# Sigmoid attention and a two-layer MLP: quarter matmuls gathered beside every second block, and PSUM banks shared between scores and sums

## The chip, the cores and the metric

The kernel runs on one core of a Trainium2 chip. The metric is the time of the program on the device in microseconds, the median of the runs shown. Engines: TensorE (PE; its weight loads are listed as PEld), VectorE (DVE), ScalarE (ACT), GpSimd (POOL), SyncE (SP), which issues the DMAs.

## The reference

Batch 8, 12 heads, sequence 448, head dimension 64; then an MLP of 768 x 2048 x 768 over the 3584 rows.

```python
scores = scale * np.matmul(q, k.transpose(0, 1, 3, 2)) - np.log(S)
attn = 1.0 / (1.0 + np.exp(-scores))
x = np.matmul(attn, v)                # heads joined: (3584, 768)
h = x @ w_in
r = np.maximum(h, 0.0)
out = (r * r) @ w_out
```

## The kernel before, in words

The kernel has two parts. The first, of about 252 us, is the attention, and beside it the conversion of the MLP's weights (they arrive as 64-bit words) into float32 blocks and the sums that the second part needs. The second part, the MLP, multiplies in a seven-product scheme; the change does not touch it.

The attention runs over 48 pairs of heads. A block `d` (0 to 23) treats the pairs `n = 2d` and `n + 1`. The order of the instructions on each engine is that of the program text, written out by hand; a tile waits for a free buffer of its kind, and each engine's queue is in order.

The 448 keys of a head are three tiles of 128 and a rest of 64. TensorE does four kinds of work in a block, in three forms:

- scores (`scores`, tile `sc`, L276): two heads side by side, each on 64 of the 128 rows ("64*128"). Six score tiles per block, three for each pair, of two PSUM banks each; three passes for each tile, `qh qh`, `qh ql`, `ql qh`: x is split into a high and a low part. A sigmoid on ScalarE (L259) reads each tile out into `at`.
- the scores of the rests (`scores_rest`, tile `sr`, L292): quarters, "64*64", for the two pairs of the *next* block, with a sigmoid of their own into `rest`.
- the rests' part of the sums (`attn_v_rest`, tile `pav`, L304): quarters, which open the sums of this block.
- the sums over the full key tiles (`attn_v`, tile `pav`, L313): halves, "128*64", 24 records a block.

PSUM has eight banks: three score tiles of two banks (tag `sc`) and one tile `duo` of two, which takes one score tile of each block (the fourth) and then the block's two sums. The next block begins with `put`: VectorE copies the two sums out (L322, `xo`).

VectorE does in each block, in this order: a step of the weight conversion (`weights_join`), the high part of one x (`high`, L489), the two copies (`put`), its low part (`low`, L493), at some blocks parts of the MLP's operands (`later`, `pieces`), a second high part, a second step of conversion, its low part. Steps of the conversion are numbered `k`; of three, two are conversions (`convert_join`, L152, L153, L156 on VectorE, then an add on GpSimd, L159), and one makes the four sums of a block of weights (`sums`, L168 to L171), which read what GpSimd added. ScalarE does the first half of a conversion (`convert_words`, L147, L148). `weights_of(piece, n)` runs the steps that fall on pair `n`: nearly always one.

SyncE's queue takes the loads of x (five to six pairs ahead), of v (one block ahead), of the weights, and the stores. x, v, `at`, `rest` and the high and low parts share 35 buffers (`op2`).

Before the loop, eight matmuls on zeros run while the first x is loaded (in two pieces).

Of the kernel before, what the change touches and what calls it, by code (L numbers as in the profile page):

```python
# [8 lines left out]
F32 = mybir.dt.float32  # L9
# [6 lines left out]
PSUM = bass.MemoryType.PSUM  # L16

B, H, S, D = 8, 12, 448, 64
DM, DFF = H * D, 2048
P = 128  # L20
# [42 lines left out]
DEFERRED = (5, 6, 7)  # L63


PIECES = {12: (1,), 14: (2,), 18: (3,), 21: (6,)}
T_PIECES = {17: ("t1",), 21: ("t2",), 23: ("t3",)}


# [1 line left out]
def sigmoid_attention_relu2_mlp(  # L71
# [171 lines left out]

    def load_pair(b, p):
        x = op2(f"x_{b}_{p}")
        to, src = (t.rearrange("p a s -> p (a s)") for t in (x, qk[b, p]))

        for at, end in ((0, S + P), (S + P, 2 * S)) if (b, p) == (0, 0) else ((0, 2 * S),):
            nc.sync.dma_start(out=to[:, at:end], in_=src[:, at:end])
        return x  # L250

    def load_v(b, d):
        vt = op2(f"v_{b}_{d}").rearrange("p a s -> p (a s)").rearrange("p (t d) -> p t d", d=P)
        nc.sync.dma_start(out=vt, in_=v[b, d])
        return vt

    def sigmoid(name, sc):
        at = op2(name)
        nc.scalar.activation(at, sc, AF.Sigmoid, bias=NEG_LOG_S, scale=SCALE)  # L259
        return at  # L260

    def score_tile(name):
        return ps.tile([P, 2, 512], F32, tag="sc", bufs=3, name=name)[:, :, :S]

    def scores(b, p, x, passes=((0, 0), (1, 0), (0, 1))):

        out = []

        other = (0, 2) if (b, p) >= (B - 1, NP - 2) else (1, 0)
        for t in range(NT):  # L270
            sc = (duo if (p % 2, t) == other else score_tile)(f"sc_{b}_{p}_{t}")
            ks = slice(t * P, (t + 1) * P)
            for n, (kp, qp) in enumerate(passes):
                for j in range(2):
                    rows = slice(j * D, (j + 1) * D)
                    nc.tensor.matmul(  # L276
                        sc[:, j],
                        x[kp][rows, 1, ks],
                        x[qp][rows, 0],
                        start=(n == 0),  # L280
                        stop=(n == len(passes) - 1),
                    )
            out.append(sigmoid(f"at_{b}_{p}_{t}", sc))
        return out

    def scores_rest(d, xs):

        sc = score_tile(f"sr_{d}")
        for r, x in enumerate(xs):
            for j in range(2):  # L290
                rows = slice(j * D, (j + 1) * D)
                nc.tensor.matmul(  # L292
                    sc[r * KR : (r + 1) * KR, j], x[rows, 1, NT * P :], x[rows, 0], start=True, stop=True
                )
        return sigmoid(f"rest_{d}", sc)

    def attn_v_rest(d, rest, vt):

        sums = duo(f"pav_{d}")
        pavs = [sums[:, r] for r in range(2)]  # L300
        for r in range(2):
            for j in range(2):
                rows, columns = slice(r * KR, (r + 1) * KR), slice(j * D, (j + 1) * D)
                nc.tensor.matmul(  # L304
                    pavs[r][columns], vt[rows, 2 * NT, columns], rest[rows, j], start=True, stop=False
                )
        return pavs

    def attn_v(n, pav, at, vt):
        for t in range(NT):  # L310
            for j in range(2):
                columns = slice(j * D, (j + 1) * D)
                nc.tensor.matmul(  # L313
                    pav[columns], vt[:, n % 2 * NT + t, columns], at[t][:, j], start=False, stop=(t == NT - 1)
                )

    def put_x(b, p, pav, scalar=False):
# [114 lines left out]
    def block(d):  # L432

        n = 2 * d
        more = n + 2 <= last
        for m in (n + 5, n + 6):
            load(m)
        if more:  # L440
            vt[d + 1] = load_v(*divmod(d + 1, NP // 2))
        for store in ready:
            store()
        ready.clear()
        if d == 0:
            for m in (1, 2, 3):
                high(m)
                low(m)
            score(0, (x[0],), ((0, 0),))
            rest[0] = scores_rest(0, (x[0], x[1]))  # L450
        else:
            weights_of(weights_join, n - 2)
            high(n + 3)
            put(n - 2)
            put(n - 1)
            low(n + 3)
            for piece in later:
                piece()
            later.clear()
            pieces_of(*T_PIECES.get(d, ()))  # L460
            score(n, xs[n])
        score(n + 1, xs[n + 1])
        if more:
            rest[d + 1] = scores_rest(d + 1, (x[n + 2], x[n + 3]))
        pav[n], pav[n + 1] = attn_v_rest(d, rest.pop(d), vt[d])
        for m in (n + 2, n + 3):
            weights_of(weights_load, m)
        high(n + 4)
        weights_of(weights_join, n - 1)
        low(n + 4)  # L470
        for m in (n, n + 1):
            weights_of(weights_words, m)
        if more:
            for store in stores:
                store()
            stores.clear()
        attn_v(n, pav[n], at[n], vt[d])
        attn_v(n + 1, pav[n + 1], at[n + 1], vt[d])
        for name in PIECES.get(d, ()):
            pieces[name](later)  # L480

    def load(n):
        if n <= last:
            x[n] = load_pair(*pairs[n])

    def high(n):
        if n <= last:
            xs[n] = op2(f"qh_{n}", F32R), op2(f"ql_{n}", F32R)
            nc.vector.tensor_copy(out=xs[n][0], in_=x[n])  # L489

    def low(n):
        if n <= last:
            nc.vector.tensor_sub(out=xs[n][1], in0=x[n], in1=xs[n][0].bitcast(F32))  # L493
# [7 lines left out]
    def weights_of(piece, n):  # L501
        for k in range(NK):
            if k * NWP // NK == n:
                piece(k)
# [19 lines left out]
    def duo(name):  # L524
        return ps1.tile([P, 2, 512], F32, tag="duo", bufs=1, name=name)[:, :, :S]
# [218 lines left out]
        return ahead  # L744

    with tc.manual_schedule():
        with tc.tile_pool(name="ps", bufs=3, space=PSUM) as ps:
            wp = ps.tile([P, 2, 512], F32, tag="sc", bufs=3, name="warm_ps")[:, :, :S]
            for i in range(8):
                nc.tensor.matmul(wp[:, 0], warm[:, :P], warm[:, :S], start=True, stop=True)  # L750
            load(0)
            load(1)
            vt[0] = load_v(0, 0)
            load(2)
            load(3)
            for k in range(2):
                weights_load(k)
            load(4)
            for d in range(len(pairs) // 2 - 2):
                block(d)  # L760
                if d == KEPT * NP // 2:
                    ops[0], made = x_operands(0)
                    pieces.update(made)
            load_first(0, False)
            block(len(pairs) // 2 - 2)
            load_first(0, True)
            for i in (1, 2):
                load_first(i, False)
            halve_weights(first[0, False])
            block(len(pairs) // 2 - 1)  # L770
            halve_weights(first[1, False])
            put(last - 1)
            put(last, True)
        ps2 = ctx.enter_context(tc.tile_pool(name="ps2", bufs=6, space=PSUM))
        work = [
            (0, lambda: pieces_of(7)),
            (1, lambda: halve_weights(first[0, True])),
            (2, lambda: pieces_of(5)),
            (4, lambda: halve_weights(first[2, False])),
            (5, lambda: pieces_of("t4")),  # L780
            (6, lambda: pieces_of(4)),
            (9, lambda: [store() for store in stores]),
        ]
        at_step = {s: n for n, s in enumerate(STEPS[0])}

        for (n, i), (j, late), wait in (
            [((7, 0), (1, True), 4), ((7, 1), (3, False), 4), ((4, 0), (2, True), 4)]
            + [((7, i), (i + 2, False), 4) for i in range(2, NI - 2)]
            + [((4, i), (i + 2, True), 4 if i < NI - 3 else 2) for i in range(1, NI - 2)]
        ):  # L790
            at_load = at_step[n, i]
            work.append((at_load, lambda j=j, late=late: load_first(j, late)))
            work.append((at_load + wait, lambda j=j, late=late: halve_weights(first[j, late])))
        for n, i in enumerate(DEFERRED):
            work += deferred(i, 10 + 12 * n)
        between = {}
        for n, piece in work:
            between.setdefault(n, []).append(piece)
        made = gemm1(0, ops[0], first, between)
# [40 lines left out]
```

## Time and profile before

| | |
|---|---|
| median of 3 runs | 1075.53 us (1075.03 to 1076.74) |
| the profiled execution | 1074.75 us, span 1072.9 us |
| TensorE busy | 1066.6 us, 99% |
| VectorE, ScalarE, GpSimd busy | 777.7, 608.8, 75.3 us |
| the attention, to the MLP's first matmul | 251.91 us |

Rows of a timeline give the start in us from the span's start, the duration from the first start to the last end of the merged instructions, engine, line, operation, tiles, shapes and count, and in brackets the idle time of the engine before it with what ended it. A matmul of these types is recorded more than once for each call in the code, and records overlap: the time that a step costs is the distance from start to start. "64*128" is the part of the array that a matmul uses, rows by columns.

### The profile page before, as it was taken

The numbers are of one execution on the slowest core, as the hardware profiler recorded it, in microseconds if no ns is written. First come the engines' busy times: TensorE is split into PE (matmuls) and PEld (weight loads), VectorE is DVE, ScalarE is ACT, GpSimd is POOL, SyncE is SP. The second block draws the span as 40 slices with busy tenths as digits, with TensorE's granted clock in tenths as the row PEclk, the third lists the DMA queues.
The fourth block names the chain that finished last, engine by engine and source line by source line (L and its number), as shares of the span: only waits on it lengthen the run. The fifth ranks groups of instructions, "written<-read, shape, count | busy, mean of one in ns | idle before, by whom it ended". The sixth has DMA issues, their size and how long they took to land.

```text
span 1072.9 us, 14947 instructions
## 1 busy us (share of the span) xinstructions
PE 1066.6 (99%) x5858; PEld 888.7 (83%) x5858; DVE 777.7 (72%) x888; ACT 608.8 (57%) x749; POOL 75.3 (7%) x42
## 2 busy tenths in 40 slices
PE   9999999999999999999999999999999999999998
PEld 4555555557999999999999999999999999999997
DVE  6888899876688898635579884456997925579941
ACT  6877778766766765433455654334565523455721
POOL 1322232210121000000000000000000000000000
PEclk9999999999999999999999999999999999999999
DMA  9989999791566445533342465333335633333441
GB/s 363 387 291 329 366 381 336 297 304 55 195 240 212 144 143 170 189 123 104 103 140 83 147 221 179 107 105 104 106 127 195 203 98 122 120 97 112 144 144 52
DMA packets 83446, 196.80 MB, mean 183 GB/s; under 512 B 6704, under 2 KB 57776, under 8 KB 83376
## 3 DMA queue, kind: packets, MB, share of 16 engines
q1 hardware_dynamic: 83376, 195.85, 52.9%
q8 instruction: 46, 0.75, 0.3%
q14 instruction: 24, 0.20, 0.1%
HBM read 154.53 MB, written 41.29 MB: 183 GB/s over the span
## 4 chain that ended last, share of the span: by engine, by line
PE 81%; DVE 2%; issue 0%; POOL 0%; ACT 0%; DVEq 0%; ACTq 0%
PE ha L534 22%; PE oa L534 22%; PE hb L534 11%; PE ob L534 11%; PE hc L534 5%; PE oc L534 5%; PE pav L313 2%; PE sc L276 2%; PE pav L304 0%; PE sr L292 0%; DVE a L152 0%; POOL a L159 0%; DVE qh L489 0%; DVE xo L322 0%; DVE ql L493 0%
## 5 line engine op out<-in xcount | busy, mean ns | idle before, releaser
L237 DVE TENSOR_TENSOR w_1l<-w_1l,w_1h 128x1536 fp32r<-128x1536 f32 x60 | 105.9, 1765 | 73.6 <-ACT w_1h L236 73.0
L259 ACT ACTIVATE at<-sc 128x896 f32<-128x896 f32 x144 | 119.6, 934 | 57.8 <-PE sc L276 57.8
L577 ACT COPY s<-ha 128x448 f32<-128x448 f32 x96 | 50.9, 531 | 132.2 <-PE ha L534 122.1
L313 PE MATMUL pav<-at,v 128*64 128x448 f32 x576 | 113.5, 543 | 0.0
L236 ACT CAST w_1h<-w_1l 128x1536 fp32r<-128x1536 f32 x60 | 88.8, 1481 | 19.2 <-DMA w_1l<-w 18.9
L313 PEld LDWEIGHTS pav<-at,v 128*64 128x64 f32 x576 | 39.2, 137 | 72.7 <-issue 71.0
L237 DVE TENSOR_TENSOR w_5l<-w_5l,w_5h 128x1152 fp32r<-128x1152 f32 x32 | 43.3, 1354 | 45.0 <-ACT w_5h L236 45.0
L159 POOL TENSOR_TENSOR a<-a,f 128x768 int32<-128x768 int32 x26 | 60.8, 2340 | 162.8 <-DVE a L156 52.5
L236 ACT CAST w_0h<-w_0l 128x1536 fp32r<-128x1536 f32 x28 | 41.5, 1481 | 50.6 <-DMA w_0l<-w 50.6
L237 DVE TENSOR_TENSOR w_0l<-w_0l,w_0h 128x1536 fp32r<-128x1536 f32 x28 | 49.1, 1755 | 19.4 <-ACT w_0h L236 19.3
L276 PE MATMUL sc<-qh 64*128 64x448 f32 x282 | 54.6, 383 | 1.6 <-DVE xo L322 1.6
L493 DVE TENSOR_TENSOR ql<-x,qh 128x896 fp32r<-128x896 f32 x47 | 54.8, 1166 | 0.1
L276 PE MATMUL sc<-qh,ql 64*128 64x448 f32 x282 | 51.8, 362 | 0.0
L276 PE MATMUL sc<-ql,qh 64*128 64x448 f32 x282 | 51.6, 361 | 0.0
L236 ACT CAST w_5h<-w_5l 128x1152 fp32r<-128x1152 f32 x32 | 37.1, 1159 | 25.2 <-DMA w_5l<-w 25.1
L614 DVE TENSOR_TENSOR g<-hb,s 128x448 f32<-128x448 f32 x32 | 19.9, 622 | 43.3 <-PE hb L534 43.3
L276 PEld LDWEIGHTS sc<-qh 64*128 64x128 f32 x282 | 26.7, 184 | 21.4 <-issue 14.7
L560 DVE SCALAR_TENSOR_TENSOR g<-g 128x896 f32<-128x896 f32 x40 | 43.6, 1090 | 1.1
L489 DVE CAST qh<-x 128x896 fp32r<-128x896 f32 x47 | 32.4, 690 | 8.5 <-DMA x<-qk 8.5
L702 ACT COPY t<-oa 128x448 f32<-128x448 f32 x36 | 19.1, 529 | 31.8 <-PE oa L534 31.5
L322 DVE COPY xo<-pav 128x448 f32<-128x448 f32 x47 | 27.2, 619 | 12.4 <-PE pav L313 12.2
L534 PE MATMUL oa<-o_0h,w_0h 128*128 128x448 f32 x96 | 35.1, 365 | 0.0
(522 smaller groups left out, 3062.0 us busy)
## 6 DMA issues: line engine op xcount, KB each, us to landing
w_1l<-w SPq DMA_DIRECT2D x60, 768.0 KB, 4.5
w_0l<-w SPq DMA_DIRECT2D x28, 768.0 KB, 4.5
x<-qk SPq DMA_DIRECT2D x47, 448.0 KB, 7.0
f<-w_in SPq DMA_DIRECT2D x16, 768.0 KB, 7.7
w_5l<-w SPq DMA_DIRECT2D x32, 384.0 KB, 3.9
v<-v SPq DMA_DIRECT2D x24, 448.0 KB, 7.4
outT<-o SPq DMA_DIRECT2D x47, 224.0 KB, 2.1
w<-s SPq DMA_DIRECT2D x13, 768.0 KB, 8.9
```

The source lines that it names most:

```text
L159: nc.gpsimd.tensor_tensor(out=wb, in0=wb, in1=t.bitcast(I32)[:, :, 0], op=ALU.add)
L236: nc.scalar.copy(out=hi, in_=raw)
L237: nc.vector.tensor_sub(out=lo, in0=raw, in1=hi.bitcast(F32))
L259: nc.scalar.activation(at, sc, AF.Sigmoid, bias=NEG_LOG_S, scale=SCALE)
L276: nc.tensor.matmul(sc[:, j], x[kp][rows, 1, ks], x[qp][rows, 0], start=(n == 0), stop=(n == len(passes) - 1),)
L313: nc.tensor.matmul(pav[columns], vt[:, n % 2 * NT + t, columns], at[t][:, j], start=False, stop=(t == NT - 1))
L322: nc.vector.tensor_copy(out=x, in_=pav)
L489: nc.vector.tensor_copy(out=xs[n][0], in_=x[n])
L493: nc.vector.tensor_sub(out=xs[n][1], in0=x[n], in1=xs[n][0].bitcast(F32))
L534: nc.tensor.matmul(out, a[:, c], b, start=first and n == 0, stop=last and n == 2, skip_group_check=True)
L560: nc.vector.scalar_tensor_tensor(out=t, in0=t, scalar=0.0, in1=t, op0=ALU.max, op1=ALU.mult)
L577: nc.scalar.copy(out=s, in_=banks["a", i])
```

## The change

- Quarters: those of four pairs run together, behind the halves of every even block: scores of the rests for blocks `d + 2` and `d + 3`, then the rests' part that closes the sums of block `d` and the part that opens those of `d + 1`. An odd block has no quarters. Blocks 0 and 1 begin this in a way of their own.
- Banks: two score tiles (`sc`) instead of three, and two tiles of sums: `even` and `odd` (the former `duo`), for the blocks of even and odd number. `LENT` says which of the six score tiles of a block (0 to 5) take one of them: in an even block the third takes `even` and the fourth `odd`; in an odd block, where `odd` holds opened sums, the third and the sixth take `even`.
- VectorE's order: the two copies come first in a block. The steps of the conversion move: three in an even block (one ahead of the first low part, two around the second high part), one in an odd one; on ScalarE one word step in an even block and three in an odd one. High and low parts are made one pair later, for the next block's pairs only.
- Loads: x is loaded eight and nine pairs ahead instead of five and six (blocks 0 and 1 load four each), v two blocks ahead instead of one. The first x comes in one piece, and there are nine matmuls on zeros.
- One piece of the MLP's operands moves from block 21 to 22.

```diff
-PIECES = {12: (1,), 14: (2,), 18: (3,), 21: (6,)}
+PIECES = {12: (1,), 14: (2,), 18: (3,), 22: (6,)}
...
     def score_tile(name):
-        return ps.tile([P, 2, 512], F32, tag="sc", bufs=3, name=name)[:, :, :S]
+        return ps.tile([P, 2, 512], F32, tag="sc", bufs=2, name=name)[:, :, :S]
+
+    def even(name):
+        return ps.tile([P, 2, 512], F32, tag="even", bufs=1, name=name)[:, :, :S]
+
+    def odd(name):
+        return duo(name)
+
+    LENT = {0: {2: even, 5: odd}, 1: {2: odd, 3: even}, 2: {2: even, 3: odd}, 3: {2: even, 5: even}}
...
-        other = (0, 2) if (b, p) >= (B - 1, NP - 2) else (1, 0)
+        d, at = divmod(b * NP + p, 2)
         for t in range(NT):
-            sc = (duo if (p % 2, t) == other else score_tile)(f"sc_{b}_{p}_{t}")
+            sc = LENT.get(min(d, 2 + d % 2), {}).get(at * NT + t, score_tile)(f"sc_{b}_{p}_{t}")
...
         n = 2 * d
-        more = n + 2 <= last
-        for m in (n + 5, n + 6):
+        for m in {0: (4, 5, 6, 7), 1: (8, 9, 10, 11)}.get(d, (n + 8, n + 9)):
             load(m)
-        if more:
-            vt[d + 1] = load_v(*divmod(d + 1, NP // 2))
+        for e in {0: (1,), 1: (2, 3)}.get(d, (d + 2,)):
+            if 2 * e <= last:
+                vt[e] = load_v(*divmod(e, NP // 2))
...
-            weights_of(weights_join, n - 2)
-            high(n + 3)
             put(n - 2)
             put(n - 1)
-            low(n + 3)
+            high(n + 2)
+            weights_of(weights_join, n - 2 if d % 2 else n - 3)
+            low(n + 2)
...
-        if more:
-            rest[d + 1] = scores_rest(d + 1, (x[n + 2], x[n + 3]))
-        pav[n], pav[n + 1] = attn_v_rest(d, rest.pop(d), vt[d])
         for m in (n + 2, n + 3):
             weights_of(weights_load, m)
-        high(n + 4)
-        weights_of(weights_join, n - 1)
-        low(n + 4)
-        for m in (n, n + 1):
-            weights_of(weights_words, m)
+        if d % 2 == 0:
+            weights_of(weights_words, n)
+            weights_of(weights_join, n - 2)
+            high(n + 3)
+            weights_of(weights_join, n - 1)
+        else:
+            for m in (n - 1, n, n + 1):
+                weights_of(weights_words, m)
+            high(n + 3)
+        low(n + 3)
...
-        attn_v(n, pav[n], at[n], vt[d])
-        attn_v(n + 1, pav[n + 1], at[n + 1], vt[d])
+        opens = n not in pav
+        if opens:
+            open_sums(d)
+        for m in (n, n + 1):
+            attn_v(m, pav[m], at[m], vt[d], opens)
         for name in PIECES.get(d, ()):
             pieces[name](later)
+        for e in {0: (1,), 1: (2, 3)}.get(d, () if d % 2 else (d + 2, d + 3)):
+            if 2 * e <= last:
+                rest[e] = scores_rest(e, (x[2 * e], x[2 * e + 1]))
+        if opens:
+            attn_v_rest((pav[n], pav[n + 1]), rest.pop(d), vt[d], False)
+        if d % 2 == 0 and d:
+            open_sums(d + 1)
+            attn_v_rest((pav[n + 2], pav[n + 3]), rest.pop(d + 1), vt[d + 1], True)
+
+    def open_sums(d):
+        sums = (odd if d % 2 else even)(f"pav_{d}")
+        pav[2 * d], pav[2 * d + 1] = sums[:, 0], sums[:, 1]
```

More of the change, by code (lines that the diff above doesn't have):

```diff
@@ L245, in load_pair @@
         x = op2(f"x_{b}_{p}")
-        to, src = (t.rearrange("p a s -> p (a s)") for t in (x, qk[b, p]))
-        for at, end in ((0, S + P), (S + P, 2 * S)) if (b, p) == (0, 0) else ((0, 2 * S),):
-            nc.sync.dma_start(out=to[:, at:end], in_=src[:, at:end])
+        nc.sync.dma_start(out=x, in_=qk[b, p])
         return x
@@ L286, in scores_rest @@
     def scores_rest(d, xs):
-        sc = score_tile(f"sr_{d}")
+        sc = (score_tile if d else odd)(f"sr_{d}")
         for r, x in enumerate(xs):
@@ L295, in scores_rest, with attn_v_rest @@
         return sigmoid(f"rest_{d}", sc)
-    def attn_v_rest(d, rest, vt):
-        sums = duo(f"pav_{d}")
-        pavs = [sums[:, r] for r in range(2)]
+    def attn_v_rest(pavs, rest, vt, opens):
         for r in range(2):
@@ L304, in attn_v_rest, with attn_v @@
                 nc.tensor.matmul(
-                    pavs[r][columns], vt[rows, 2 * NT, columns], rest[rows, j], start=True, stop=False
+                    pavs[r][columns], vt[rows, 2 * NT, columns], rest[rows, j], start=opens, stop=not opens
                 )
-        return pavs
-    def attn_v(n, pav, at, vt):
+    def attn_v(n, pav, at, vt, opens):
         for t in range(NT):
@@ L313, in attn_v @@
                 nc.tensor.matmul(
-                    pav[columns], vt[:, n % 2 * NT + t, columns], at[t][:, j], start=False, stop=(t == NT - 1)
+                    pav[columns],
+                    vt[:, n % 2 * NT + t, columns],
+                    at[t][:, j],
+                    start=opens and t == 0,
+                    stop=not opens and t == NT - 1,
                 )
@@ L445, in block @@
         if d == 0:
-            for m in (1, 2, 3):
-                high(m)
-                low(m)
+            high(1)
+            low(1)
             score(0, (x[0],), ((0, 0),))
@@ L462, in block @@
         score(n + 1, xs[n + 1])
-        if more:
-            rest[d + 1] = scores_rest(d + 1, (x[n + 2], x[n + 3]))
-        pav[n], pav[n + 1] = attn_v_rest(d, rest.pop(d), vt[d])
+        if d == 0:
+            high(2)
+            low(2)
         for m in (n + 2, n + 3):
             weights_of(weights_load, m)
-        high(n + 4)
-        weights_of(weights_join, n - 1)
-        low(n + 4)
-        for m in (n, n + 1):
-            weights_of(weights_words, m)
-        if more:
+        if d % 2 == 0:
[8 more added lines that the diff above has]
+        low(n + 3)
+        if n + 2 <= last:
             for store in stores:
@@ L746, in sigmoid_attention_relu2_mlp @@
     with tc.manual_schedule():
-        with tc.tile_pool(name="ps", bufs=3, space=PSUM) as ps:
-            wp = ps.tile([P, 2, 512], F32, tag="sc", bufs=3, name="warm_ps")[:, :, :S]
-            for i in range(8):
+        with tc.tile_pool(name="ps", bufs=2, space=PSUM) as ps:
+            wp = score_tile("warm_ps")
+            for i in range(9):
                 nc.tensor.matmul(wp[:, 0], warm[:, :P], warm[:, :S], start=True, stop=True)
@@ L757, in sigmoid_attention_relu2_mlp @@
                 weights_load(k)
-            load(4)
             for d in range(len(pairs) // 2 - 2):
```

## The prediction

> **What bounds the kernel now.** I read the page's part 1 first, then TensorE's (PE's) row in the waits, then the timeline of one block in the middle of the attention part, engine by engine.
>
> ```profile
> PE 1066.6 (99%) x5858; PEld 888.7 (83%) x5858; DVE 777.7 (72%) x888; ACT 608.8 (57%) x749; POOL 75.3 (7%) x42
> ```
> ```profile
> PE sc L276 <- DVE xo L322: 1.6, 2, 0.8
> ```
> ```profile
> 107.97 0.47 PE L276 MATMUL sc<-qh 64*128 64x448 f32 x2
> 108.28 0.36 PE L276 MATMUL sc<-qh,ql 64*128 64x448 f32 x2
> 108.48 0.36 PE L276 MATMUL sc<-ql,qh 64*128 64x448 f32 x2
> ...
> 111.52 0.36 PE L276 MATMUL sc<-ql,qh 64*128 64x448 f32 x2
> 111.81 0.98 PE L292 MATMUL sr<-x 64*64 64x448 f32 x8
> 112.61 0.93 PE L304 MATMUL pav<-rest,v 64*64 64x448 f32 x8
> 113.47 4.73 PE L313 MATMUL pav<-at,v 128*64 128x448 f32 x24
> 118.13 0.47 PE L276 MATMUL sc<-qh 64*128 64x448 f32 x2
> ```
>
> TensorE is busy 99% of the span and hardly waits: the waits name two of 0.8 us on the copies of the sums (`xo`, L322), and that is all behind the start. So every microsecond is one of TensorE's order of work; the other engines count only where they make it wait. The block from 107.97 to 118.13 takes 10.16 us, and the reader is to see its four parts: 18 steps of two score matmuls side by side (64*128), then the quarters (64*64) of the scores and of the sums, 8 records each, then 24 records of halves (128*64).
>
> ```profile
> 11.99 0.14 PEld L313 LDWEIGHTS pav<-at,v 128*64 128x64 f32 x2 [0.23 <-issue]
> ...
> 15.38 0.14 PEld L313 LDWEIGHTS pav<-at,v 128*64 128x64 f32 x2 [0.23 <-issue]
> ```
>
> A score step takes (111.52 - 108.48) / 15 = 0.203 us, one of the sums (15.38 - 11.99) / 9 = 0.377 us, and a group of four quarters about the same (two of them from 111.81 to 112.61). The work alone is 18 x 0.203 + 12 x 0.377 + 4 x 0.377 = 9.68 us. The other 0.48 us lies at the three changes of form (scores to quarters, quarters to halves, halves to scores): 0.16 us each.
>
> **The change part by part.**
>
> *Fewer changes of form.* The work of TensorE stays the same. From block 2 on, an even block runs scores, halves, 32 records of quarters; an odd one scores and halves alone: five changes in two blocks where there were six. Blocks 0 and 1 keep five and three, the last goes from three to two. 74 become 63, at 0.16 us: **-1.8 us**. Scores straight to halves, and halves straight to quarters, do not occur in this trace; between nothing and the 0.31 us of the slowest score step behind a change (107.97 to 108.28) they are nearest the mean of the three seen. Ends: 0 and -3.4 us. By these terms an even block takes 9.68 + 1.51 + 0.48 = 11.67 us, an odd one 9.68 - 1.51 + 0.32 = 8.49.
>
> *Copies of x first.* In two blocks the fourth score tile waited for the copies of the last sums, which stood behind a join and a cast on VectorE.
>
> ```profile
> 190.90 1.15 DVE L322 COPY xo<-pav 128x448 f32<-128x448 f32 x2
> 191.02 0.37 PE L276 MATMUL sc<-ql,qh 64*128 64x448 f32 x2
> 192.19 0.47 PE L276 MATMUL sc<-qh 64*128 64x448 f32 x2 [0.80 <-DVE xo L322]
> 192.47 0.40 PE L276 MATMUL sc<-qh,ql 64*128 64x448 f32 x2
> ```
>
> The copies ended at 192.05 and the matmul started 0.14 us later; its step then took 0.28 instead of 0.20. The whole wait cost 192.19 - 191.02 - 0.20 + 0.08 = 1.05 us, twice: **-2.1 us**. Now the copies are first in a block. Behind an odd block, whose VectorE queue is short (below), they start 0.12 us after the first score (the trace has 0.11: 108.08) and let TensorE go at 0.12 + 1.15 + 0.14 = 1.41 us; the tile that needs them is the fourth, due at 0.10 + 3 x 0.61 = 1.93 us. Nothing is late there.
>
> *Two score tiles and one lent, in odd blocks.* A score tile is three steps, 0.61 us. Before, four tiles went round. Now the odd block holds the opened sums of its own pairs in one of the two sum tiles, and its six score tiles go through three places: A, B, even, A, B, even. So the fourth to sixth wait for the sigmoids of the first to third.
>
> ```profile
> L259 ACT ACTIVATE at<-sc 128x896 f32<-128x896 f32 x144 | 119.6, 934 | 57.8 <-PE sc L276 57.8
> ```
> ```profile
> 108.94 4.97 ACT L259 ACTIVATE at<-sc 128x896 f32<-128x896 f32 x6 [2.74 <-PE sc L276]
> 113.74 0.98 ACT L259 ACTIVATE rest<-sr 128x896 f32<-128x896 f32 x1
> 114.53 1.00 ACT L147 ACTIVATE a<-f 128x768 f32<-128x768 f32 x1
> 115.36 0.99 ACT L148 ACTIVATE f<-f 128x768 int32<-128x768 uint32 x1
> ```
>
> Sigmoids start 0.97 us behind the block's first score (108.94 - 107.97) and follow at (113.74 - 108.94) / 6 = 0.80 us, 0.93 each; ScalarE is idle ahead of them. They end at 1.90, 2.70 and 3.50 us; with the 0.14 us of the row above (measured on VectorE's copies; ScalarE's price is not in the trace) the places are free at 2.04, 2.84 and 3.64. The fourth tile is due at 1.93, so it waits 0.11; the fifth would then start at 2.73 (a step of 0.28 in it) and waits until 2.84, the sixth until 3.64 instead of 3.14. With its own longer step that is 0.58 us. Without any delay behind the sigmoid it is 0.36. Odd blocks from 3 on are eleven: **+6.4 us**, ends 4.0 and 8. In even blocks four tiles go round as before: the fifth is due at 2.54, its place free at 2.04. ScalarE's two word conversions of an odd block (0.83 us each half, 3.3 in all) run from about 5.9 to 9.2 us, when the next block begins, 0.97 us ahead of its first sigmoid; they cost nothing.
>
> *Three joins in an even block.* VectorE had two steps of weight conversion in every block; now it has three in an even one (two conversions and a set of sums, in an order that turns) and one in an odd one.
>
> ```profile
> 100.52 0.55 DVE L152 TENSOR_SCALAR a<-a 128x768 f32<-128x768 f32 x1
> 101.11 0.56 DVE L153 TENSOR_SCALAR a<-a 128x768 int32<-128x768 int32 x1
> 101.71 0.96 DVE L156 SCALAR_TENSOR_TENSOR a<-f,a 128x768 int32<-128x768 int32 x1
> 102.58 1.09 DVE L493 TENSOR_TENSOR ql<-x,qh 128x896 fp32r<-128x896 f32 x1
> 103.58 2.22 DVE L152 TENSOR_SCALAR a<-a 128x768 f32<-128x768 f32 x1
> 105.83 0.56 DVE L153 TENSOR_SCALAR a<-a 128x768 int32<-128x768 int32 x1
> 106.43 0.96 DVE L156 SCALAR_TENSOR_TENSOR a<-f,a 128x768 int32<-128x768 int32 x1
> 107.31 0.62 DVE L489 CAST qh<-x 128x896 fp32r<-128x896 f32 x1
> 108.08 1.16 DVE L322 COPY xo<-pav 128x448 f32<-128x448 f32 x2 [0.16 <-PE pav L313]
> ...
> 111.07 0.54 DVE L168 TENSOR_TENSOR s<-a 128x384 f32<-128x384 f32 x1
> ...
> 113.06 1.08 DVE L493 TENSOR_TENSOR ql<-x,qh 128x896 fp32r<-128x896 f32 x1
> ```
> ```profile
> 102.90 2.49 POOL L159 TENSOR_TENSOR a<-a,f 128x768 int32<-128x768 int32 x1 [7.69 <-DVE a L156]
> ```
> ```profile
> 122.04 0.96 DVE L156 SCALAR_TENSOR_TENSOR a<-f,a 128x768 int32<-128x768 int32 x1
> ...
> 125.74 0.56 DVE L168 TENSOR_TENSOR s<-a 128x384 f32<-128x384 f32 x1 [1.74 <-POOL a L159]
> ```
>
> By starts: two copies 1.07 us, a cast 0.54, a conversion 2.06 (100.52 to 102.58), a low part 1.0, sums 1.99 (111.07 to 113.06). Two things stretch these. A conversion that begins while GpSimd's add of the last one runs has its first instruction at 2.22 us instead of 0.55 (103.58; the add runs 102.90 to 105.39): from L156 of the one to L153 of the other 105.83 - 101.71 = 4.12 us. And sums behind a conversion wait for that add, 125.74 - 122.04 = 3.70 us from its L156.
>
> [...]
>
> An even block's queue, from its start: copies to 1.19, cast to 1.73, first join, low part, second join, cast, third join, low part. In blocks 2, 10 and 18 the joins are conversion, conversion, sums: L156 at 2.91, L153 of the second at 7.03, its L156 at 7.62, GpSimd's add at 8.7 (1.09 later, as at 122.04), sums from 10.9 (a cast alone beside the add), low part from 12.9, done at 13.9. The odd block begins at 11.67. Its copies, first in the block but behind all this, start at 13.9 and let TensorE go at 15.2, 3.5 us into the block; the third score tile, lent from those sums, was due at 1.32. The sixth waits for that tile's sigmoid, 0.91 + 0.93 + 0.14 = 1.98 us later, and so starts at 5.5 instead of 3.14: 2.4 us for the block, 1.9 beyond the 0.58 already counted. Three times: +5.6 us. With sums between two conversions (blocks 4, 12, 20) the queue ends at 12.2 and the third tile starts at 1.8 (0.2 us more each); with sums first (6, 14, 16) it ends at 12.05, 0.05 more; block 8 has two joins, 22 one. Together **+6.3 us**, ends 0 (queue in time everywhere) and 12 (every odd block as late as the worst third on average).
>
> *The start.* Nine warming matmuls for eight, and the first x whole.
>
> ```profile
> 1.15 3.17 PE L750 MATMUL warm_ps<-warm 128*128 128x448 bf16 x8 [1.15 <-DVE warm L396]
> 4.25 2.55 PE L276 MATMUL sc<-x 64*128 64x448 f32 x12
> ```
>
> A warming matmul steps by 0.37 us, so the ninth ends its step at 4.49 where the scores began at 4.25: +0.25 us, given back because the quarters that now come behind the halves do not wait for the third and fourth x. Zero, ends -0.5 and +0.5.
>
> *Loads four pairs earlier.* SyncE's queue carries the same bytes; x and v stand further ahead, weights a little later. Costed at nothing: words are converted a block later than their load. The cover is gone if the 35 two-row buffers, of which I count 27 held in an odd block and up to 36 with the operands of blocks 12 to 18, stop the queue for long.
>
> **Sum.** -1.8 - 2.1 + 6.4 + 6.3 + 0 = +8.8 us on the profiled execution's 1074.75 us (span 1072.9): 1083.5. The median of the runs is 0.8 above that execution, so the forecast for it is **1084 us**.
>
> **The rivals.** *VectorE in time:* casts and sums overlap better than the rows above, and only the three places bind: -3.9 + 6.4 = +2.5, 1078. For it: the odd blocks leave VectorE nearly 3 us idle each, and it was in time in 22 of 24 blocks; against: no row shows three joins in 11.7 us. *Faster:* the three places do not bind, because the first of the three is late by only 0.11 us by my sum, all of it the borrowed 0.14; if ScalarE's release is earlier than its row's end by 0.4 us and VectorE is in time, -3.9 us remain: 1071.6. It decides below 0.35 us for an odd block (3.9 / 11). Against it: 0.80 us for a sigmoid against 0.61 for a tile. *Buffers:* the queue of loads or ScalarE waits for one of the 35, from block 12 on: bounded by 0.80 us (one sigmoid) and 2.74 us (ScalarE's idle time ahead of a block's sigmoids, used up) in six blocks, 4.8 to 16.4 us on top of the forecast: 1089 to 1100.
>
> **How the numbers follow.** Forecast (1079 to 1088) 0.62; VectorE in time 0.16; faster 0.10; buffers 0.12. The range 1077 to 1091 takes the first two and half of the last. A difference under 0.2% (2.2 us) can't be told from none; the second rival lies at +0.23%, so part of it is "same": faster 0.10, same 0.10, slower 0.80.
>
> **What would show it.** Changes of form: even blocks of 11.7 us, odd ones of 8.5 with no wait in them. Places: TensorE waiting on the sigmoid in each odd block, its score part 4.3 to 4.4 us instead of 3.84. VectorE: waits of the third score tile on the copies in blocks 3, 11 and 19, about 2.2 us each, behind a low part that ends near 13.9 us. The two waits of 0.8 us gone. Wrong if odd blocks stay near 8.5 us, or if loads show as a wait.

## The result: slower, 1088.47 us against 1075.49

The changed kernel takes 1088.47 us (median of 6 runs, 1087.95 to 1088.76), the kernel before beside it 1075.49: 1.0117 times as long (95% interval 1.0103 to 1.0132), +13.0 us. The profiled execution took 1088.76 us, its span 1087.0, 14.1 more than before. All of it lies in the attention: the MLP's first matmul starts at 266.06 us where it started at 251.91, and the MLP behind it takes 820.9 us where it took 821.0.

First TensorE's line of the page, and its row in the waits, of the changed kernel:

```profile
PE 1073.2 (99%) x5859; PEld 891.8 (82%) x5859; DVE 786.2 (72%) x888; ACT 611.6 (56%) x749; POOL 77.9 (7%) x42
```
```profile
PE sc L284 <- DVE xo L331: 9.1, 9, 2.0
```

The share of busy time is the same 99%. The waits on the copies of the sums have grown from 1.6 us in two places to 9.1 us in nine, of up to 2.0 us.

The timeline of TensorE from an even block in time (block 8, with the gathered quarters) to the end of the score part of an odd one (block 9), and ScalarE's beside the odd block:

```profile
93.82 0.47 PE L284 MATMUL sc<-qh 64*128 64x448 f32 x2
...
97.65 4.73 PE L318 MATMUL pav<-at,v 128*64 128x448 f32 x24
102.31 1.73 PE L300 MATMUL sr<-x 64*64 64x448 f32 x16
103.86 1.68 PE L310 MATMUL pav<-rest,v 64*64 64x448 f32 x16
105.48 0.47 PE L284 MATMUL sc<-qh 64*128 64x448 f32 x2
...
107.43 0.47 PE L284 MATMUL sc<-qh 64*128 64x448 f32 x2
107.74 0.37 PE L284 MATMUL sc<-qh,ql 64*128 64x448 f32 x2
107.95 0.37 PE L284 MATMUL sc<-ql,qh 64*128 64x448 f32 x2
108.24 0.47 PE L284 MATMUL sc<-qh 64*128 64x448 f32 x2
...
109.05 0.47 PE L284 MATMUL sc<-qh 64*128 64x448 f32 x2
...
109.86 4.73 PE L318 MATMUL pav<-at,v 128*64 128x448 f32 x24
```
```profile
106.46 4.97 ACT L256 ACTIVATE at<-sc 128x896 f32<-128x896 f32 x6 [1.31 <-PE sc L284]
111.26 0.95 ACT L147 ACTIVATE a<-f 128x768 f32<-128x768 f32 x1
```

The even block takes 105.48 - 93.82 = 11.66 us, with no wait in it. In the odd block the fourth, fifth and sixth tile start at 107.43, 108.24 and 109.05: 0.81 us apart, the sigmoids' 0.80 (106.46 to 111.26, six), not the 0.61 of three score steps. The score part takes 109.86 - 105.48 = 4.38 us instead of 3.84. These stops are too short for the waits' list; one sees them in the distance of the starts, and in the first step of each tile, 0.31 us where others take 0.20.

Now block 3, where the copies are late: VectorE from block 2 on, then TensorE, with the waits of blocks 11, 14 and 19 below.

```profile
28.02 1.16 DVE L331 COPY xo<-pav 128x448 f32<-128x448 f32 x2 [6.36 <-PE pav L310]
...
31.68 1.08 DVE L522 TENSOR_TENSOR ql<-x,qh 128x896 fp32r<-128x896 f32 x1
32.68 2.21 DVE L152 TENSOR_SCALAR a<-a 128x768 f32<-128x768 f32 x1
34.93 0.56 DVE L153 TENSOR_SCALAR a<-a 128x768 int32<-128x768 int32 x1
...
38.75 0.56 DVE L168 TENSOR_TENSOR s<-a 128x384 f32<-128x384 f32 x1 [1.73 <-POOL a L159]
...
40.76 1.08 DVE L522 TENSOR_TENSOR ql<-x,qh 128x896 fp32r<-128x896 f32 x1
41.76 1.15 DVE L331 COPY xo<-pav 128x448 f32<-128x448 f32 x2
```
```profile
40.68 0.37 PE L284 MATMUL sc<-ql,qh 64*128 64x448 f32 x2
43.05 0.47 PE L284 MATMUL sc<-qh 64*128 64x448 f32 x2 [2.01 <-DVE xo L331]
43.33 0.55 PE L284 MATMUL sc<-qh,ql 64*128 64x448 f32 x2
43.62 0.64 PE L284 MATMUL sc<-ql,qh 64*128 64x448 f32 x2
43.99 0.64 PE L284 MATMUL sc<-qh 64*128 64x448 f32 x2
...
129.69 0.47 PE L284 MATMUL sc<-qh 64*128 64x448 f32 x2 [2.01 <-DVE xo L331]
...
160.76 0.47 PE L284 MATMUL sc<-qh 64*128 64x448 f32 x2 [0.74 <-DVE xo L331]
...
216.05 0.47 PE L284 MATMUL sc<-qh 64*128 64x448 f32 x2 [2.00 <-DVE xo L331]
```

The queue of block 2 begins at 28.02 and reaches the next copies 13.74 us later; they let TensorE go at 43.05, 3.50 us into block 3 (39.55). And behind the wait there is something new: from 43.6 us on, a score step takes 0.37 us instead of 0.20. The windows have it (length; busy time of PE, PEld, DVE, ACT, POOL with their counts; granted clock; DMA's share and GB/s):

```profile
43.42:46.83 3.41, 3.41 (x22) 3.41 (x20) 3.34 (x6) 2.13 (x3) 1.20 (x1) 0.50 0.95 323
...
129.68:132.40 2.72, 2.71 (x26) 2.22 (x26) 2.65 (x5) 1.80 (x3) 0.04 (x1) 1.00 1.02 419
217.50:220.91 3.41, 3.41 (x17) 2.15 (x16) 3.38 (x3) 3.21 (x5) 2.28 (x1) 0.50 1.05 432
```

Behind the waits of 2.0 us in blocks 3 and 19 the granted clock is 0.50 for 3.41 us; behind the one in block 11, just as long, it stays at 1.00.

In one block it is ScalarE that is late. Its rows around the start of block 6 (72.76):

```profile
71.22 0.94 ACT L147 ACTIVATE a<-f 128x768 f32<-128x768 f32 x1 [1.53 <-POOL a L159]
...
74.47 4.91 ACT L256 ACTIVATE at<-sc 128x896 f32<-128x896 f32 x6
```

The word steps of block 5 wait 1.53 us for GpSimd's add, and run on into block 6: its sigmoids begin 1.71 us behind the first score instead of 0.97, and the fifth and sixth tile wait for them.

Where the 14.1 us are, summed from the starts of the parts of every block (a score part in time takes 3.84 us):

| | predicted | measured |
|---|---|---|
| three places in eleven odd blocks (0.54 each) | +6.4 | +5.9 |
| late copies (6.3 in odd blocks, 2.0 in blocks 14 and 22, small rests) | +6.3 | +8.6 |
| late sigmoids in block 6 | 0 | +0.4 |
| half clock, two stretches of 1.5 us lost | 0 | +3.0 |
| eleven changes of form less | -1.8 | -1.8 |
| old waits on the copies (two of 1.1 us; 0.2 us each in blocks 1 and 23) | -2.1 | -2.6 |
| to the start of block 1 (16.23 to 16.96) | 0 | +0.7 |
| sum | +8.8 | +14.2 |

### The profile page after: what moved, and what is told of

The parts are those of the page before. It is cut to its first block, busy times and chain, and to the rows that moved or that the text cites. A ratio compares the mean times of both kernels' runs of the same rounds, so it can differ in the third digit from the quotient of the medians.

```text
span 1087.0 us, 14940 instructions
## 1 busy us (share of the span) xinstructions
PE 1073.2 (99%) x5859; PEld 891.8 (82%) x5859; DVE 786.2 (72%) x888; ACT 611.6 (56%) x749; POOL 77.9 (7%) x42
## 4 chain that ended last, share of the span: by engine, by line
PE 82%; DVE 3%; issue 1%; POOL 0%; ACT 0%; DVEq 0%; ACTq 0%; POOLq 0%
PE ha L563 21%; PE oa L563 21%; PE hb L563 11%; PE ob L563 11%; PE hc L563 5%; PE oc L563 5%; PE pav L318 3%; PE sc L284 3%; DVE xo L331 1%; DVE ql L522 1%; DVE a L152 1%; POOL a L159 0%; PE pav L310 0%; DVE a L153 0%; DVE qh L518 0%
## 5 line engine op out<-in xcount | busy, mean ns | idle before, releaser
L159 POOL TENSOR_TENSOR a<-a,f 128x768 int32<-128x768 int32 x26 | 63.4, 2440 | 180.3 <-DVE a L156 95.1
L284 PE MATMUL sc<-qh 64*128 64x448 f32 x282 | 58.9, 405 | 9.1 <-DVE xo L331 9.1
L284 PE MATMUL sc<-ql,qh 64*128 64x448 f32 x282 | 54.0, 369 | 0.0
L522 DVE TENSOR_TENSOR ql<-x,qh 128x896 fp32r<-128x896 f32 x47 | 51.1, 1088 | 1.1
L589 DVE SCALAR_TENSOR_TENSOR g<-g 128x896 f32<-128x896 f32 x40 | 43.6, 1090 | 1.1
L518 DVE CAST qh<-x 128x896 fp32r<-128x896 f32 x47 | 39.4, 838 | 5.3 <-DMA x<-qk 5.3
L637 ACT ACTIVATE g<-ha 128x448 f32<-128x448 f32 x32 | 17.4, 544 | 31.7 <-PE ha L563 31.7
```

Of the source, the lines that this page charges most:

```text
L159: nc.gpsimd.tensor_tensor(out=wb, in0=wb, in1=t.bitcast(I32)[:, :, 0], op=ALU.add)
L284: nc.tensor.matmul(sc[:, j], x[kp][rows, 1, ks], x[qp][rows, 0], start=(n == 0), stop=(n == len(passes) - 1),)
L589: nc.vector.scalar_tensor_tensor(out=t, in0=t, scalar=0.0, in1=t, op0=ALU.max, op1=ALU.mult)
```

## The experiments

A join is one step of the weight conversion on VectorE, a place one PSUM tile that takes scores. The theory when the experiments were made: the loss is the three places, VectorE's queue of three joins in even blocks, and the half clock behind its long waits. The rivals: loads and buffers, or one of the two parts alone.

**Two joins in every block.**

```diff
-weights_of(weights_join, n - 2 if d % 2 else n - 3)
+weights_of(weights_join, n - 2)
...
-if d % 2 == 0: ...                # one or three words, two joins or none
+for m in (n, n + 1):
+    weights_of(weights_words, m)
+high(n + 3)
+weights_of(weights_join, n - 1)
```

> Two steps of the weight conversion in every block on VectorE, and two word steps on ScalarE, as before the change; all else as changed. Theory (three places for scores in odd blocks cost 0.55 us each, the rest is VectorE's queue of three joins in even blocks, which delays the copies of the sums, and the half clock after the long waits): blocks 3, 11 and 19 lose their waits of 2 us, no stretch of half clock is left, odd score parts stay at 4.3 to 4.6 us; the odd blocks' own queue of about 9.9 us in 9.0 makes some even blocks 0.4 us late. 1078 to 1081 us. Rival (the loads or the buffers, not the joins, make VectorE late): the waits stay, 1085 to 1089 us.

Measured: 1079.83 us, 1.0046 of before (1.0029 to 1.0063). The waits of this kernel, and TensorE in block 14:

```profile
PE sc L284 <- DVE xo L331: 3.2, 3, 1.1
```
```profile
152.61 0.37 PE L284 MATMUL sc<-ql,qh 64*128 64x448 f32 x2
154.06 0.47 PE L284 MATMUL sc<-qh 64*128 64x448 f32 x2 [1.07 <-DVE xo L331]
```

The waits of 2 us are gone, and with them the half clock (the mean granted clock of the profiled execution is 1.000, that of the changed kernel 0.997); 8.6 us come back by moving the joins and the word steps on ScalarE that feed them, with the loads as deep as in the change. The odd score parts stay at 4.30 to 4.38 us. Three waits of 1.1 us are left, longer than the 0.4 us expected, in blocks 14, 20 and 22: behind odd blocks in which VectorE also makes operands of the MLP.

**Without GpSimd's add.**

```diff
-nc.gpsimd.tensor_tensor(out=wb, in0=wb, in1=t.bitcast(I32)[:, :, 0], op=ALU.add)
```

> The changed kernel without GpSimd's add of the weights' last bits (one instruction for each conversion is left out, so the weights lack these bits). [...] Rival (three joins are too much for VectorE by their own work): blocks 3, 11 and 19 keep over half of their waits, above 1083 us.

Measured: 1076.05 us, 1.0009 (0.9999 to 1.0018), where 1076 to 1079 us were forecast if it is the add that makes the queue late. VectorE's queue of block 2 again, three joins as in the change:

```profile
31.10 1.08 DVE L521 TENSOR_TENSOR ql<-x,qh 128x896 fp32r<-128x896 f32 x1
32.10 0.55 DVE L152 TENSOR_SCALAR a<-a 128x768 f32<-128x768 f32 x1
...
34.69 0.55 DVE L167 TENSOR_TENSOR s<-a 128x384 f32<-128x384 f32 x1
...
36.69 1.08 DVE L521 TENSOR_TENSOR ql<-x,qh 128x896 fp32r<-128x896 f32 x1
38.36 1.15 DVE L330 COPY xo<-pav 128x448 f32<-128x448 f32 x2 [0.58 <-PE pav L309]
```

The second conversion's first instruction takes 0.55 us instead of 2.21 (32.68 in the changed kernel, where an add ran from 31.90 to 34.47), the sums wait for nothing where they waited 1.73 us for the add, and the copies now wait for TensorE. So it is not three joins as such, it is GpSimd's add between them: beside it VectorE's next conversion takes 1.66 us longer, and the sums need its result. What makes the conversion longer is not shown. The copies took no longer beside an add: in the kernel before two of them took 1.16 us (from 108.08) while an add ran from 107.52 to 109.65. No wait on the copies is left; the odd score parts are 4.31 to 4.38 us. On TensorE's side this kernel has the three places, the saved changes of form and nothing else of the change; from block 1 to the MLP it takes 237.0 us, 5.7 us of them waits in score parts, against 235.7 with 2.6 before: 233.1 - 231.3 = 1.8 us for eleven changes of form, 0.16 each.

**Own rests, four places everywhere.**

```diff
-3: {2: even, 5: even}}
+3: {2: odd, 3: even}}
...
-        if d % 2 == 0 and d:
-            open_sums(d + 1)
-            attn_v_rest((pav[n + 2], pav[n + 3]), rest.pop(d + 1), vt[d + 1], True)
```

> The rests' part of the sums closes each block's own sums, behind its halves, in odd blocks too, so that in odd blocks four places take scores (third tile in odd, fourth in even); the scores of the rests stay together for four pairs; three joins in even blocks stay. Eleven more changes of form. Theory: odd blocks in time have score parts of 3.84 us (0.55 less, eleven times, -6.0), eleven changes of form at 0.16 come back (+1.8), late copies in blocks 3, 11 and 19 stay, now at the fourth tile: 1083 to 1086 us. Rival (the places do not bind; the score part of 4.38 us comes from late copies alone): score parts of odd blocks stay above 4.2 us, and the time rises by 1.8 us to 1090.

Measured: 1090.19 us (four runs, 1088.26 to 1103.50), 1.0165 (1.0105 to 1.0225); with this spread the time can't be told from the changed kernel's. A miss of the theory's time, and the rival's number; but its trace speaks against the rival. Block 9, then the waits, then the clock behind two of them:

```profile
107.45 0.36 PE L284 MATMUL sc<-ql,qh 64*128 64x448 f32 x2
107.66 0.37 PE L284 MATMUL sc<-qh 64*128 64x448 f32 x2
...
109.57 0.97 PE L318 MATMUL pav<-at,v 128*64 128x448 f32 x3
```
```profile
PE sc L284 <- DVE xo L331: 9.9, 10, 2.2
```
```profile
44.38:47.79 3.41, 3.41 (x17) 2.09 (x16) 3.34 (x5) 2.75 (x3) 1.68 (x1) 0.50 0.96 368
218.46:221.87 3.41, 3.41 (x18) 2.33 (x16) 3.34 (x5) 2.80 (x4) 1.56 (x1) 0.50 1.04 426
```

Where the copies are in time the tiles follow without a gap, score part 3.84 us: the places did bind. What the expectation forgot is that the even block loses eight records of quarters (0.75 us) while its queue of three joins stays, so its copies are later by as much. Summed as in the table, late copies cost about 13 us here instead of 8.6, which takes back most of the 5.9 us of the places.

**Both.**

> Both edits: two joins in every block, and each block's own rests close its sums, with four places for scores everywhere. Theory: nothing waits, -2.2 us against the kernel before for the two waits that are gone, no gain from changes of form (as many as before): 1073 to 1076 us, the start up to 0.7 us later. Rival (the deeper loads cost time too): above 1078 us.

Measured: 1078.2 us, 1.0012 (0.9969 to 1.0055). Above the theory's range and just above the rival's threshold. Odd score parts are 3.84 us; three waits on the copies, of up to 1.5 us, in blocks 14, 20 and 22, account for the difference to the expectation (1.7 us each with the longer steps behind them); the next version tests it. The odd block, now 9.4 us long, holds two joins and the MLP's operands.

**Both, the MLP's operands one block earlier.**

```diff
-PIECES = {12: (1,), 14: (2,), 18: (3,), 22: (6,)}
-T_PIECES = {17: ("t1",), 21: ("t2",), 23: ("t3",)}
+PIECES = {11: (1,), 13: (2,), 17: (3,), 21: (6,)}
+T_PIECES = {16: ("t1",), 20: ("t2",), 23: ("t3",)}
```

> As the version with two joins in every block and own rests, and besides the MLP's operands are made one block earlier (pieces in blocks 11, 13, 17, 21, two of the subtractions in blocks 16 and 20), so that VectorE's part of them falls in the longer even blocks. Theory: the three waits of 1.5 us on the copies in blocks 14, 20 and 22 go: 1073 to 1075 us, below the kernel before. Rival (those waits come from the loads' depth or the start): 1077 us or more.

Measured: 1075.70 us, 1.0006 (0.9997 to 1.0014), between the theory's range and the rival's. The long waits went, four of up to 0.3 us came elsewhere; no gain over the kernel before, with the loads as deep as in the change.

**Two joins and the operands earlier, quarters gathered.**

> The changed kernel with two joins in every block and the MLP's operands one block earlier, with the quarters gathered and three places in odd blocks as changed. Theory: the three waits of 1.1 us on the copies go, the eleven of 0.5 us on the sigmoids stay (+5.6), eleven changes of form are saved (-1.8) and the two old waits (-2.2): 1075 to 1077 us, no gain over the kernel before. Rival (gathering is worth more once nothing is late): below 1074 us.

Measured: 1077.15 us, 1.0018 (1.0009 to 1.0027), at the upper end of the theory. Gathering with nearly nothing late still does not pay: the odd score parts take 4.31 to 4.38 us.

**Three places in the kernel before.**

```diff
-sc = (duo if (p % 2, t) == other else score_tile)(...)
+sc = (duo if (p % 2, t) == other and (b * NP + p) // 2 % 2 == 0 else score_tile)(...)
```

> The kernel before with one place less for scores in odd blocks: their fourth tile (in the last block the third) takes one of the three score tiles instead of the tile of sums. Theory (three places in a rotation cost 0.5 us, because a sigmoid takes 0.80 us and a tile 0.61): twelve odd blocks with score parts of 4.3 to 4.5 us instead of 3.84, 1081 to 1083 us. Rival (TensorE's wait was due to the copies' place in the queue, not to the number of tiles): within 1 us of the kernel before.

Measured: 1079.89 us, 1.0043 (1.0029 to 1.0057). TensorE in block 9 of this kernel:

```profile
100.20 0.47 PE L276 MATMUL sc<-qh 64*128 64x448 f32 x2
...
102.15 0.47 PE L276 MATMUL sc<-qh 64*128 64x448 f32 x2
...
102.96 0.48 PE L276 MATMUL sc<-qh 64*128 64x448 f32 x2
...
103.77 0.47 PE L276 MATMUL sc<-qh 64*128 64x448 f32 x2
...
104.58 0.61 PE L292 MATMUL sr<-x 64*64 64x448 f32 x4
```

The same picture as in block 9 of the changed kernel, 0.81 us from tile to tile, 4.38 us in all, with nothing else of the change: the price of the three places by itself. The time is 1 us below the expected range, since the old waits in blocks 18 and 20 shrink where VectorE has more time.

**Copies first, in the kernel before.**

```diff
-            weights_of(weights_join, n - 2)
-            high(n + 3)
             put(n - 2)
             put(n - 1)
+            weights_of(weights_join, n - 2)
+            high(n + 3)
             low(n + 3)
```

> The kernel before with one part of the change alone: the two copies of the sums stand first in VectorE's block. Theory: the two waits of 1.05 us on the copies go, nothing else moves: 1073 to 1074 us. Rival (the join that now stands behind the copies makes a later step late): 1075 us or more.

Measured: 1076.36 us, 1.0008 (0.9996 to 1.0020). No gain: a miss. Of the old waits the one in block 18 went, the one in block 20 grew from 0.8 to 1.1 us, and two of 0.6 us came in blocks 14 and 22. Its waits, then TensorE and VectorE around block 20:

```profile
PE sc L276 <- DVE xo L322: 2.3, 3, 1.1
```
```profile
214.34 0.47 PE L276 MATMUL sc<-qh 64*128 64x448 f32 x2 [1.08 <-DVE xo L322]
```
```profile
207.85 1.15 DVE L333 TENSOR_TENSOR x_0l<-xo,x_0h 128x448 fp32r<-128x448 f32 x2
...
212.04 1.08 DVE L493 TENSOR_TENSOR ql<-x,qh 128x896 fp32r<-128x896 f32 x1
213.05 1.15 DVE L322 COPY xo<-pav 128x448 f32<-128x448 f32 x2
```

The copies stand first in the block, but the queue of the block before ends 1.9 us into it (block 20 starts at 211.17): what stood ahead of the copies in their own block now stands behind those of the block before, and is ahead of them all the same.

**Copies first, the MLP's operands in blocks with fewer conversions.**

```diff
-PIECES = {12: (1,), 14: (2,), 18: (3,), 21: (6,)}
-T_PIECES = {17: ("t1",), 21: ("t2",), 23: ("t3",)}
+PIECES = {11: (1,), 14: (2,), 16: (3,), 21: (6,)}
+T_PIECES = {15: ("t1",), 20: ("t2",), 23: ("t3",)}
```

> The kernel before with the copies of the sums first in VectorE's block and the MLP's operands made in other blocks (pieces in 11, 14, 16, 21, two of the subtractions in 15 and 20), where fewer weight conversions stand beside them. Theory (a wait on the copies is set by how late VectorE's whole queue ends a block, not by the copies' place in it): no wait on the copies is left, 1073 to 1074 us. Rival (the start and other run-to-run parts hide it, or the waits move once more): 1075 us or more.

Measured: 1074.35 us, 0.9991 (0.9982 to 1.0000). Apart from one at the start, on a low part, the waits name none on the copies:

```profile
PE sc L276 <- DVE ql L493: 0.4, 1, 0.4
```

The fastest version of all, by about 1 us, though the interval reaches to no gain and the time lies 0.35 us above the expected range; in five blocks the fourth tile is still 0.2 to 0.3 us late, too little for the list.

## Why the prediction was right, and what it mis-sized

The sign, the places of the loss and the range held; the median lies 4.5 us above the point, and just above the 1079 to 1088 of the forecast's own case. The terms that were missing fell into the upper part of the range, which had been left for the rival on buffers: that it held them is in part luck.

- *Fewer changes of form*: right in size, -1.8 us, from the mean of three changes, two of which the new order does not have. It is borne out: an even block in time takes 11.66 us (predicted 11.67), and an odd one is 3.84 + 4.66 = 8.50 us beside its waits (predicted 8.49).
- *Three places*: right, 0.54 us for 0.58, and shown alone in the kernel before. The release behind a sigmoid (about 0.05 us in block 9) is faster than the borrowed 0.14 us, so the sixth tile starts at 3.57 us instead of 3.64; its first step is longer than assumed, 0.31 us instead of 0.28.
- *Three joins*: right in cause and place. The queue of block 2 reached the next copies 13.74 us after its own; the prediction had 13.9 - 0.12. The cause is shown by leaving the add out: 0.55 us for 2.21, and no wait on the copies. The odd blocks came to the 6.3 us of the term. It was mis-sized by 2.3 us, mainly because of "Nothing is late there" for the copies behind an odd block: blocks 14 and 22 were 1.0 us late each, behind odd blocks in which VectorE also makes the MLP's operands, which the prediction had costed nowhere.
- *ScalarE's word conversions*: "they cost nothing" failed in block 6, where they had waited 1.53 us for GpSimd's add and made the sigmoids late. +0.4 us.
- *The half clock* was missing altogether: the step "2.4 us for the block" took TensorE to go on at full speed behind a wait of 2 us; in blocks 3 and 19 the granted clock was 0.50 for 3.41 us. +3.0 us.
- *Copies first, -2.1 us*: the old waits did go, but not by this step. Alone it brought no gain; a wait on the copies is set by when VectorE's whole queue ends the block (1.9 us into the next in block 20 there, a wait of 1.08).
- *The start*: +0.7 us in this execution. Over the eleven kernels profiled, block 1 starts at 16.23 to 16.92 us with the old start and at 15.97 to 17.44 with the new one, so no price of the change is shown. The old start alone in the changed kernel was not tried.
- *Loads four pairs earlier*: nothing, as costed; the versions with deep loads and no late copies stand at the kernel before. The rival on buffers is not seen.
- The rival *Faster* asked for less than 0.35 us in an odd block; it was 0.54. The rival *VectorE in time* came true in the version without the add: 1076.05, where it said 1078.

## What to carry to other kernels

Before saving a 0.16 us change of form, count what it takes from the rotation of PSUM tiles: where the reader takes 0.80 us for each of six tiles that TensorE fills in 0.61, a fourth place hides the difference and a third pays it, 0.54 us a block. Work moved between the blocks of an in-order queue must be added up for each block, with the neighbours that it meets there (in block 2 an add on GpSimd between two conversions cost 1.66 us, 2.21 for 0.55, and the sums' wait for the next add 1.73); the average over two blocks says nothing. And what made the head of a block late here was mostly the tail of the block before.

## What the runs showed of the hardware

- Behind some waits of TensorE of 2 us the granted clock was 0.50 for 3.41 us. In the changed kernel it happened behind two of three such waits: in block 3 from 43.42 us on, 0.37 us after TensorE had resumed (43.05), and in block 19 from 217.50, 1.45 us after (216.05), but not in block 11, where the wait ended at 129.69 and the clock was 1.00 up to 138.00. By the table the two cost 3.0 us beside the waits, about 1.5 each. With own rests, whose longest wait is 2.2 us, there are two such stretches too, 44.38 to 47.79 and 218.46 to 221.87. In *Both*, whose longest wait is 1.5 us, the mean granted clock of the profiled execution is 0.999, against 0.997 in the two kernels with the stretches. What decides which wait is followed by one was not shown.
- All twelve conversions on VectorE that began while GpSimd's add ran, six in the kernel before and six in the changed one, took 2.20 to 2.23 us for their first instruction; the other forty of that shape took 0.55 to 0.56.
- TensorE follows the end of a VectorE copy by 0.14 to 0.15 us (42.91 to 43.05 in block 3, 215.90 to 216.05 in block 19) and that of a sigmoid by about 0.05 (in block 9 the second and third sigmoid end at 108.19 and 109.00, and the fifth and sixth tile start at 108.24 and 109.05).
